# Redistributing K, Q and the selection mask inside the chip, instead of by extra reads of PSUM and by transfers

## The chip, the core and the metric

The kernel runs on one core of a Trainium2 chip. The metric is the device time of the program in microseconds, where less is better. [...] An instruction that waits for a semaphore holds all that follows it on its engine.

## What is computed

For 4 batches and 8 heads of width 64 over 768 positions, each query picks 6 of 24 chunks of 32 keys by an upper bound on its scores, and attends causally to those alone. The heads side by side then go through a two-layer network with an ELU between its layers.

```python
k_min = np.min(k_chunks, axis=3); k_max = np.max(k_chunks, axis=3)
ub = sum_d(maximum(q * k_min, q * k_max))          # per query and chunk
ub = where(causal, ub, -1e9); top_chunks = argsort(ub)[..., -6:]
scores = where(selected & causal, q @ k.T / 8, -1e9)
attn = softmax(scores); x = heads_side_by_side(attn @ v)     # 3072 x 512
h = x @ w_in                                       # 512 -> 2048
out = where(h > 0, h, exp(min(h, 0)) - 1) @ w_out  # 2048 -> 512
```

## The kernel before

The work is cut into eight units (batch b, half h of the sequence), in the order (0,0), (0,1), (1,0) and so on. A unit has four head pairs r. For each pair `prep` loads K, Q and V of the half (384 positions, both heads side by side in the free dimension), transposes K and Q on PE so that head 0 lies in partitions 0 to 63 and head 1 in 64 to 127 of a PSUM bank (`tr`, L383), and reduces the K bank to the chunk minima and maxima (`red`, two reductions on DVE, L392).

The scores need one operand per head with the mask beside it. `lhsA` holds K of head 0 in the lower 64 partitions and constant mask rows (`econst`, -40000 where a key's chunk is the row's chunk) in the upper 64. `lhsB` holds K of head 1 in the upper half and mask rows in the lower one. `rhsA` and `rhsB` hold Q in the same way with a 0/1 row per chunk, one where the chunk is not selected, so that one product of 128 rows gives the masked scores. K and Q are written straight from PSUM: `ka`, `kb`, `qa`, `qb` (helper `evac`, L404 on ACT, L406 on DVE), and Q a third time as a float copy `qt` (L438) with its positive part `qr` (L443, DVE) for the upper bound. A bank that one engine reads is not read by another at the same time, so the reductions on DVE and the evacuations on ACT of one bank take turns.

`select` works on two pairs. PE forms the bounds (L468) from `qt`, `qr` and `kst`, the padded minima and differences that POOL writes in 4 small instructions per pair (L418, L422). DVE transposes (L478), takes the eight largest of each query (`max`, L487), compares (L493) and transposes back (L499) into `selT`. Four transfers on the SP queue then bring the rows of `selT` to the partitions where `rhsA` and `rhsB` want them.

`attend` forms scores (L530), exponentials (ACT, L542, L548), the triangular mask on the diagonal blocks (DVE, L557, L565), the product with V (L584), the normalisation (DVE, L595, L598), a transpose (L609) and a copy to `xt` (DVE, L614). `mlp` takes the four `xt` of a unit: 16 blocks of the first layer on PE (L626), exp on ACT (L634), `m` on POOL (L638), `gT` on DVE (L642), then the second layer on PE (L653), a copy out of PSUM (L661, L663) and the store.

What is issued when is set by a list scheduler in the program: every operation has costs on the engines that may do it and a priority, `Graph.run` walks a model of the engines, and the instructions are emitted in the order found. Attention of a unit has priorities spread over 10 or 19 units of model time, and the MLP of unit i starts at 14 + 15.1 i, so MLP blocks and later attention are interleaved. Loads are issued ahead on SP, in the same order list; a weight chunk is loaded from POOL after a given cast of V (L451, POOL).

Ahead of all that `consts` sets up the identity, the triangle, the mask rows and the tiles. On DVE this is 39 instructions: 8 memsets of `kst`, 8 copies of mask rows into `lhsA` and `lhsB` (L299, POOL does 8 more) and 20 memsets of the mask halves of `rhsA` and `rhsB` among them.

Of the kernel before, what the change touches and what calls it, by code (L numbers as in the profile page):

```python
# [19 lines left out]
S = 768  # L20
# [32 lines left out]

# [6 lines left out]
class Graph:  # L60
# [40 lines left out]
    def run(self, dma_lat=(700.0, 1300.0)):  # L101
        free = {n: [(0.0, s) for s in range(len(v))] for n, v in self.slots.items()}
        engines = (PE, ACT, DVE, POOL, SP)
        at = {e: 0.0 for e in engines}
        avail = {e: [] for e in engines}
        events = [0.0]
# [9 lines left out]
        while left:  # L116
# [12 lines left out]
            while moved:  # L129
                moved = False  # L130
                for e in engines:
# [5 lines left out]
                    while i < len(lst):  # L137
# [27 lines left out]
                    for b in o.bufs:  # L165
# [48 lines left out]
def kernel(  # L214
# [24 lines left out]
    slots("kf", 6, [P, 3, 2, D], F32)  # L239
    slots("qf", 6, [P, 3, 2, D], F32)  # L240
    slots("vf", 6, [P, 3, 2, D], F32)
    slots("lhsA", 8, [P, S], BF16)
    slots("lhsB", 8, [P, S], BF16)
    slots("vext", 8, [P, 6, 2, D + 1], BF16)
    for h in range(2):
        slots(f"rhsA{h}", 5, [P, HS], BF16)
        slots(f"rhsB{h}", 5, [P, HS], BF16)
    slots("kst", 8, [P, 2, 64], F32)
# [19 lines left out]
    econst = const.tile([P, NCH, CHUNK], BF16, name="econst")  # L268
# [9 lines left out]

    def consts():
        nc.gpsimd.memset(ident_f, 0.0)  # L280
        nc.gpsimd.affine_select(out=ident_f, in_=ident_f, compare_op=AOT.not_equal,
                                fill=1.0, base=0, pattern=[[-1, P]], channel_multiplier=1)
        nc.vector.memset(warm, 0.0)
        nc.scalar.activation(out=warm, in_=warm, func=AF.Exp)
        nc.vector.memset(econst, MASKNEG)
        for r0 in (0, 64):
            nc.gpsimd.affine_select(out=econst[r0:r0 + 64], in_=econst[r0:r0 + 64],
                                    compare_op=AOT.is_equal, fill=0.0, base=0,
# [3 lines left out]
                                fill=0.0, base=0, pattern=[[1, P]], channel_multiplier=-1)  # L292
        nc.vector.tensor_copy(out=ident_b, in_=ident_f)
        for t in store["kst"]:
# [31 lines left out]
    for i in range(8):  # L326
        att_at.append(att_at[-1] + ATT_W[i % 2])
    W_GATE = [2, 3, 4, 5, 6, 7, 8, 9]
# [15 lines left out]
    vx = {}  # L344
    qq = {}
    ks = {}
    xT = {}

    def dma(dst_src, writes, reads, prio, xfer, name):
        def emit(e):  # L350
            d, s_ = dst_src()
            nc.sync.dma_start(out=d, in_=s_)
        g.op(name, c_dma(), emit, reads=reads, writes=writes, prio=prio, xfer=xfer)

    def load(b, h, r, prio):
        kf, qf, vf = g.buf("kf"), g.buf("qf"), g.buf("vf")
        for buf, src, late in ((kf, k, 0.0), (qf, q, 0.001), (vf, v, 3.0)):
            for hd in range(2):
                dma(lambda buf=buf, src=src, hd=hd: (
                        ap(buf)[:, :, hd, :],  # L360
                        src[b, 2 * r + hd, HS * h:HS * (h + 1)].rearrange("(n p) d -> p n d", p=P)),
                    [(buf, hd)], [], prio + late, 440.0, f"ld{b}{h}{r}")
        return kf, qf, vf

    def prep(b, h, r, prio):
# [32 lines left out]
        g.op("kmax" + tag, c_dve(HS), red(1, AOT.max), reads=[(bank, 0)], writes=[(kmm, 1)], prio=prio)  # L398

        def evac(eng_prio, dst, rows, cols, bk, n=HS, src0=0, name="ev"):  # L400
            def emit(e):
                o, i = ap(dst)[rows, cols], ap(bk)[rows, src0:src0 + n]
                if e == ACT:
                    nc.scalar.activation(out=o, in_=i, func=AF.Copy)  # L404
                else:
                    nc.vector.tensor_copy(out=o, in_=i)  # L406
# [314 lines left out]
```

## Time and profile before

| | |
|---|---|
| time, median of 3 runs | 331.62 us (330.03 to 333.14) |
| profiled execution | 331.95 us, its span 330.2 us |
| PE busy | 290.7 us, 88% of the span |
| DVE, ACT, POOL busy | 215.5, 213.8, 125.1 us |
| mean granted clock of PE | 0.984 |
| moved by transfers | 30.70 MB |

The span is the time from the first to the last instruction that the profiler recorded; 1.75 us of the profiled time lie around it. Busy shares are means over a start in which PE mostly waits and a long middle in which it hardly does, so the table by stretches in the section of rows says more than this one. "Idle" beside a group of instructions is the time that their engine stood still just before them, with what ended it.

### The profile page before, as it was taken

To read this page: it belongs to the slowest core of one execution; us is meant where nothing else is said; L and a number is where in the kernel's file an instruction comes from. 1 tells how busy PE (TensorE), PEld (TensorE's weight loads), DVE (VectorE), ACT (ScalarE), POOL (GpSimd) and SP (SyncE) were. 2 spreads that over 40 slices of the span, in tenths; PEclk is the share of its full clock that TensorE was granted. 3 is DMA by queue.
4 is the path that set the end of the run, shared out by engine and by line. 5 is a ranking of instruction groups with operands and counts; after the bars stand their busy time and mean duration, and the time that the engine had idled before them with its cause. 6 is when DMAs were issued, how large, how long until landed. Compare 5 with 4: busy or idle time off the path is not lost.

```text
span 330.2 us, 6933 instructions
## 1 busy us (share of the span) xinstructions
PE 290.7 (88%) x2272; PEld 172.8 (52%) x2272; DVE 215.5 (65%) x652; ACT 213.8 (65%) x477; POOL 125.1 (38%) x324
## 2 busy tenths in 40 slices
PE   4066468868999999999999999999999999999995
PEld 2044154534566656655566556656556556555542
DVE  7855877636459984686558972777589926951640
ACT  2055466943878828779759847898588685781722
POOL 8635442735136711464024600443134412520630
PEclk9997979997999999999999999999999999999999
DMA  6834999895748454504152213222110020000102
GB/s 138 186 81 76 217 195 222 149 194 118 179 108 233 106 129 119 127 9 98 47 151 53 52 48 91 65 60 48 70 37 2 2 73 32 11 2 34 64 2 95
DMA packets 86820, 30.70 MB, mean 93 GB/s; under 512 B 78848, under 2 KB 83712, under 8 KB 86784
## 3 DMA queue, kind: packets, MB, share of 16 engines
q1 hardware_dynamic: 82560, 26.07, 32.2%
q0 software_dynamic: 4224, 4.19, 8.0%
q8 instruction: 18, 0.29, 0.4%
q14 instruction: 18, 0.15, 0.2%
HBM read 27.26 MB, written 6.29 MB: 102 GB/s over the span
## 4 chain that ended last, share of the span: by engine, by line
PE 59%; DVE 16%; ACT 12%; DMA 5%; issue 4%; POOL 2%; SPq 1%; DVEq 0%; ACTq 0%; POOLq 0%
PE bank L653 23%; PE bank L626 16%; PE bank L530 6%; PE bank L383 5%; PE bank L584 4%; ACT pt L542 4%; PE bank L468 4%; DVE kmm L392 3%; DMA vf<-in_v_dram 3%; DVE gT L642 2%; DMA kf<-in_k_dram 2%; PE bank L609 2%; ACT e L634 2%; ACT lhsA L404 1%; ACT rhsA L404 1%
## 5 line engine op out<-in xcount | busy, mean ns | idle before, releaser
L626 PE MATMUL bank<-xt,w_in_sb 128*128 128x384 bf16 x512 | 94.8, 329 | 0.4 <-ACT pt L542 0.3
L638 POOL TENSOR_SCALAR m<-e 128x384 f32<-128x384 f32 x128 | 64.8, 517 | 79.7 <-ACT e L634 70.6
L653 PE MATMUL bank<-w_out_sb,gT 128*128 128x512 bf16 x384 | 93.9, 382 | 0.1
L542 ACT ACTIVATE pt<-bank 128x384 bf16<-128x384 f32 (+1 forms) x160 | 75.2, 577 | 12.4 <-PE bank L530 12.3
L642 DVE SCALAR_TENSOR_TENSOR gT<-bank,m 128x384 bf16<-128x384 f32 x128 | 67.3, 546 | 23.9 <-POOL m L638 22.2
L634 ACT ACTIVATE e<-bank 128x384 f32<-128x384 f32 x128 | 61.7, 516 | 22.1 <-PE bank L626 12.0
L626 PEld LDWEIGHTS <-w_in_sb 128*128 128x128 bf16 x512 | 48.8, 98 | 30.7 <-issue 3.4
L653 PEld LDWEIGHTS <-gT 128*128 128x128 bf16 x384 | 36.2, 98 | 36.2 <-issue 3.0
L418 POOL COPY kst<-kmm 64x12 f32<-64x12 f32 x64 | 12.6, 198 | 86.3 <-DVE kmm L392 71.6
L392 DVE TENSOR_REDUCE kmm<-bank 128x12 f32<-128x384 f32 x64 | 34.6, 551 | 14.6 <-ACT lhsA L404 9.4
L530 PE MATMUL bank<-rhsB,lhsB 128*128 128x384 bf16 x144 | 36.0, 294 | 2.0 <-DVE gT L642 0.8
L530 PE MATMUL bank<-rhsA,lhsA 128*128 128x384 bf16 x144 | 36.6, 296 | 0.9 <-DVE gT L642 0.3
L404 ACT ACTIVATE lhsA<-bank 64x384 bf16<-64x384 f32 x31 | 15.2, 491 | 23.7 <-PE bank L383 22.4
L661 ACT ACTIVATE o<-bank 128x512 f32<-128x512 f32 x20 | 11.9, 596 | 28.6 <-PE bank L653 28.5
L584 PEld LDWEIGHTS <-pt 128*128 128x128 bf16 x672 | 24.6, 97 | 9.9 <-issue 2.7
L584 PE MATMUL bank<-vext,pt 128*128 128x65 bf16 x672 | 26.9, 194 | 2.1 <-DVE pt L565 1.3
L404 ACT ACTIVATE lhsB<-bank 64x384 bf16<-64x384 f32 x30 | 14.6, 485 | 19.8 <-DVE kmm L392 18.3
L468 PE MATMUL bank<-qt,kst 128*64 128x192 f32 (+1 forms) x64 | 14.1, 448 | 14.3 <-POOL kst L418 11.9
L557 DVE TENSOR_TENSOR pt<-pt,tri 128x512 bf16<-128x512 bf16 x32 | 13.8, 432 | 17.9 <-ACT pt L542 17.9
L383 PE MATMUL bank<-ident_f,kf 128*128 128x128 f32 x96 | 18.6, 309 | 5.9 <-DMA kf<-in_k_dram 5.8
L530 PEld LDWEIGHTS <-lhsA 128*128 128x128 bf16 x144 | 14.2, 100 | 13.3 <-issue 4.9
L422 POOL TENSOR_TENSOR kst<-kmm 64x12 f32<-64x12 f32 x64 | 14.4, 224 | 15.8 <-DVE kmm L392 11.1
(55 smaller groups left out, 307.9 us busy)
## 6 DMA issues: line engine op xcount, KB each, us to landing
kf<-in_k_dram SPq DMA_DIRECT2D x64, 96.0 KB
qf<-in_q_dram SPq DMA_DIRECT2D x64, 96.0 KB
vf<-in_v_dram SPq DMA_DIRECT2D x64, 96.0 KB
out_dram<-o SPq DMA_DIRECT2D x24, 256.0 KB
w_in_sb<-in_moe_w_in_dram POOLq DMA_DIRECT2D x4, 512.0 KB, 7.3
w_out_sb<-in_moe_w_out_dram POOLq DMA_DIRECT2D x4, 512.0 KB, 7.2
rhsA<-selT SPq DMA_DIRECT2D x16, 18.0 KB
rhsB<-selT SPq DMA_DIRECT2D x16, 18.0 KB
```

The lines of the kernel that those rows point to most:

```text
L383: nc.tensor.transpose(ap(bk)[:, P * n:P * (n + 1)], ap(src)[:, n], ident_f)
L392: nc.vector.tensor_reduce(out=ap(kmm)[:, w, :], in_=ap(bank)[:, 0:HS].rearrange("p (c w) -> p c w", w=CHUNK), axis=AX.X, op=op)
L404: nc.scalar.activation(out=o, in_=i, func=AF.Copy)
L468: nc.tensor.matmul(ap(bank)[64 * j:64 * j + 64, 0:nq], lhsT=ap(ks[b, r])[:, w, :], rhs=ap(qq[b, h, r][w])[:, 0:nq], start=(w == 0), stop=( ...
L530: nc.tensor.matmul(ap(banks[hd])[:, o + pc:o + pc + wd], lhsT=ap(ls[hd])[:, P * kb:P * (kb + 1)], rhs=ap(rs[hd])[:, c0 - HS * h:c0 - HS * ...
L542: lambda e, hd=hd, pt=pt, banks=banks, wtot=wtot: nc.scalar.activation(out=ap(pt)[:, hd, 0:wtot], in_=ap(banks[hd])[:, 0:wtot], func=AF.Ex ...
L584: nc.tensor.matmul(o3v()[:, hd, qi, :], lhsT=ap(pt)[:, hd, P * qi + off:P * qi + off + P], rhs=ap(vx[b, r])[:, kb, hd, :], start=(kb == 0) ...
L626: nc.tensor.matmul(ap(bank)[:, 0:HS], lhsT=w_in_sb[:, kk, P * fc:P * (fc + 1)], rhs=ap(xT[b, h, kk]), start=(kk == 0), stop=(kk == NKK - 1))
L634: lambda e, eb=eb, bank=bank: nc.scalar.activation(out=ap(eb), in_=ap(bank)[:, 0:HS], func=AF.Exp),
L638: lambda e, eb=eb, mb=mb: nc.gpsimd.tensor_scalar(out=ap(mb), in0=ap(eb), scalar1=-1.0, scalar2=1.0, op0=AOT.add, op1=AOT.mult),
L642: lambda e, gt=gt, bank=bank, mb=mb: nc.vector.scalar_tensor_tensor(out=ap(gt), in0=ap(bank)[:, 0:HS], scalar=0.0, in1=ap(mb), op0=AOT.max ...
L653: nc.tensor.matmul(ap(bank), lhsT=ap(gts[fc])[:, P * tt:P * (tt + 1)], rhs=w_out_sb[:, fc, :], start=(fc == 0), stop=(fc == NFC - 1))
```

## The change

Six things change together.

- K and Q are read from PSUM once each, by `kt` and `qt` (all 128 partitions, ACT or DVE). Four copies per pair of 64 partitions each, SBUF to SBUF, then put K and Q of both heads into the lower partitions of one tile per pair (`lhs`, `rhs`, with a head index): `ka` on DVE or POOL, `qa` on DVE, POOL or ACT. The mask rows lie in the upper half for both heads, offset by 32 rows for head 1.
- The selection rows go from `selT` into `rhs` by one DVE copy per pair (`mk`), which shifts partitions and writes both heads. The four transfers per `select` are gone.
- `kst` is made by one subtraction (`ks`) and one multiplication with a 0/1 column (`kp`) for both heads, on DVE or POOL.
- K, Q and V of batches 1 to 3 are loaded for the whole sequence, V of both heads in one transfer and cast in one instruction. The first two Q loads are issued by ACT.
- The setup is shorter: mask rows are written into `lhs` once for each of 8 slots (`ec`, DVE), 5 memsets of `rhs` and 2 of `selb` stay on DVE, those of `kst` go to POOL, and PE gets 28 matmuls of zeros at the start.
- The scheduler starts each engine at a given time, keeps two engines from one bank at the same time, and has other costs for some operations.

```diff
-    def run(self, dma_lat=(700.0, 1300.0)):
+    def run(self, at=None, dma_lat=(900.0, 1500.0)):
...
-        at = {e: 0.0 for e in engines}
+        at = {e: (at or {}).get(e, 0.0) for e in engines}
...
+                            elif b.cls == "bank" and any(x != e and ft > t for x, ft in b.used.items()):
                                 ok = False
...
-    slots("kf", 6, [P, 3, 2, D], F32)
+    slots("kf", 3, [P, 6, 2, D], F32)
...
-    slots("lhsA", 8, [P, S], BF16)
-    slots("lhsB", 8, [P, S], BF16)
+    slots("kt", 3, [P, HS], BF16)
+    slots("lhs", 8, [P, 2, S], BF16)
...
     def consts():
+        nc.vector.memset(zeros, 0.0)
...
+        for i in range(FILL):
+            nc.tensor.matmul(store["bank"][7][:, 0:P], lhsT=zeros, rhs=zeros, start=True, stop=True)
...
+        for t in store["rhs0"]:
+            nc.vector.memset(t[up, :, 0:Q0], 0.0)
+        for t in store["kst"]:
+            nc.gpsimd.memset(t, 0.0)
...
-        for i in range(8):
-            eng = nc.vector if i < 4 else nc.gpsimd
-            for t, r in ((store["lhsA"][i], slice(64, P)), (store["lhsB"][i], slice(0, 64))):
-                eng.tensor_copy(out=t[r, :], in_=econst[r].rearrange("p c w -> p (c w)"))
...
+    FILL = 28
+    AT = {PE: 3500.0, ACT: 800.0, DVE: 3200.0, POOL: 6000.0, SP: 800.0}
...
+        elif h == 0:
+            dma(lambda: (ap(vf).rearrange("p g n d -> p (g n) d"),
+                         v[b, 2 * r:2 * r + 2].rearrange("g s d -> (g s) d")
+                         .rearrange("(m p) d -> p m d", p=P)),
...
+                g.op("ec" + tag, {DVE: (480, 560)}, ec, writes=[(lb, "e")],
...
-        evac(prio + 0.5, la, lo, ts, bank, name="ka")
-        evac(prio + 0.5, lb, hi, ts, bank, name="kb")
...
+        put("kt", lambda: ap(kt), lambda: ap(bank)[:, 0:HS], c_both(HS), [(bank, 0)], [(kt, 0)], prio)
+        for hd, rows in enumerate((lo, hi)):
+            put("ka", lambda hd=hd: ap(lb)[lo, hd, ts], lambda rows=rows: ap(kt)[rows],
+                {DVE: (175, 260), POOL: (500, 560)}, [(kt, 0)], [(lb, (h, hd))], prio + 0.5)
...
+        g.op("ks" + tag, {DVE: (85, 160), POOL: (200, 260)}, sub, reads=[(kmm, 0)], writes=[(kmm, 1)],
...
+        g.op("kp" + tag, {DVE: (115, 190), POOL: (250, 310)}, pad, reads=[(kmm, 0), (kmm, 1)],
...
-        evac(prio + 0.5, ra, lo, slice(0, HS), bq, name="qa")
-        evac(prio + 0.5, rb, hi, slice(0, HS), bq, name="qb")
...
+            put("qa", lambda hd=hd: ap(rb)[lo, hd], lambda rows=rows: ap(qt)[rows],
+                {DVE: (275, 360), POOL: (500, 560), ACT: (386, 480)}, [(qt, 0)], [(rb, hd)], prio + 0.5)
...
-            dma(lambda ra=ra, j=j: (ap(ra)[64:64 + NCH, q0:HS], ap(sT)[64 * j:64 * j + NCH, 0:nq]),
-                [(ra, "mask")], [(sT, 0)], prio, 60.0, "mk" + tag)
...
+                eng.tensor_copy(out=ap(rb)[hi, :, q0:HS],
+                                in_=ap(sT)[64 * j:64 * j + 64, 0:nq].rearrange("p (a q) -> p a q", a=1)
+                                .to_broadcast([64, 2, nq]))
+            g.op("mk" + tag, {DVE: (2 * nq / 3.84 + 75, 2 * nq / 3.84 + 160)},
...
-    order = g.run()
+    order = g.run(AT)
```

The order of the instructions moves at three places that matter below. The first is DVE from the start of the program to its first reduction of a K bank. Before:

```order
L285 MEMSET econst 128x768
L295 MEMSET kst_131 128x128
...
L299 COPY lhsA_87<-econst 64x768
L299 COPY lhsB_95<-econst 64x768
...
L302 MEMSET rhsA_111 64x192
...
L304 MEMSET rhsB_130 64x192
L392 TENSOR_REDUCE kmm_139<-bank_61 128x12 x2
L406 CAST rhsA_111<-bank_62 64x384
L443 TENSOR_SCALAR qr_146<-qt_142 128x192
```

Now, where `rhs`, `lhs` and `qt` are the new tiles:

```order
L296 MEMSET econst 64x768
L297 MEMSET econst 64x768
L300 MEMSET half 128x2
...
L311 MEMSET rhs_97 64x2x96
...
L316 MEMSET selb_130 128x192
L316 MEMSET selb_131 128x192
L418 COPY lhs_81<-econst 64x1536
...
L418 COPY lhs_87<-econst 64x1536
L492 TENSOR_SCALAR qr_122<-qt_118 128x192
L454 TENSOR_REDUCE kmm_115<-bank_62 128x12 x2
L418 COPY lhs_88<-econst 64x1536
L476 TENSOR_TENSOR kst_107<-kmm_115,half 128x4x12
```

The 8 copies of half a tile and 30 memsets ahead of the first reduction became 7 copies of twice the size and 14 memsets.

The second place is ACT on the first head pairs, where it shares the K and Q banks (61 to 64) with DVE. Before:

```order
L404 ACTIVATE lhsA_87<-bank_61 64x384
L404 ACTIVATE lhsB_95<-bank_61 64x384
L438 ACTIVATE qt_142<-bank_62 128x192
L404 ACTIVATE rhsB_116<-bank_62 64x384
L404 ACTIVATE lhsA_88<-bank_63 64x384
L404 ACTIVATE lhsB_96<-bank_63 64x384
```

Now:

```order
L441 ACTIVATE qt_118<-bank_61 128x384
L441 ACTIVATE kt_78<-bank_62 128x384
L441 ACTIVATE rhs_97<-qt_118 64x384
L441 ACTIVATE qt_119<-bank_63 128x384
L441 ACTIVATE kt_79<-bank_64 128x384
L441 ACTIVATE rhs_98<-qt_119 64x384
```

ACT reads each K bank once where it read it twice, and the third instruction of a pair reads SBUF.

The third place is the SP queue at the first two selections. Before:

```order
L352 DMA rhsA_112<-selT_156 24x192
L352 DMA rhsB_117<-selT_156 24x192
L352 DMA vf_86<-in_v_dram 128x3x64 x2
L352 DMA kf_69<-in_k_dram 128x3x64 x2
L352 DMA qf_75<-in_q_dram 128x3x64 x2
L352 DMA rhsA_113<-selT_157 24x192
L352 DMA rhsB_118<-selT_157 24x192
```

Now, at the end of batch 0 and the start of batch 1:

```order
L369 DMA qf_72<-in_q_dram 128x3x64 x2
L369 DMA vf_75<-in_v_dram 128x3x64 x2
L369 DMA kf_70<-in_k_dram 128x6x64 x2
L369 DMA qf_73<-in_q_dram 128x6x64 x2
L369 DMA vf_76<-in_v_dram 128x12x64
L369 DMA kf_71<-in_k_dram 128x6x64 x2
```

No transfer on SP reads `selT` any more; until the first store it holds loads alone.

## Rows read from the trace of the kernel before

**Rows 1.** The page's busy times: engine, us, share of the span, instructions.
```profile
PE 290.7 (88%) x2272; PEld 172.8 (52%) x2272; DVE 215.5 (65%) x652; ACT 213.8 (65%) x477; POOL 125.1 (38%) x324
```

**Rows 2.** Table by stretches: window, length, busy us, granted PE clock, DMA share, GB/s.
```profile
0.00:14.50 14.50, 3.34 (x12) 2.01 (x12) 12.13 (x39) 1.97 (x3) 11.11 (x28) 1.00 0.70 158
14.50:31.00 16.50, 10.01 (x41) 6.64 (x42) 9.48 (x36) 8.04 (x19) 5.99 (x23) 0.91 0.37 79
31.00:54.30 23.30, 14.71 (x122) 8.75 (x121) 18.04 (x54) 14.02 (x30) 10.07 (x26) 0.92 1.18 207
54.30:90.00 35.70, 29.83 (x219) 16.86 (x217) 20.28 (x63) 22.41 (x53) 15.29 (x35) 0.95 0.83 166
90.00:306.60 216.60, 212.66 (x1780) 128.17 (x1778) 146.62 (x446) 157.60 (x355) 74.67 (x198) 1.00 0.27 71
```

**Rows 3.** Timeline of the first 20 us: start, us, engine, line, what.
```profile
3.92 0.44 DVE L299 COPY lhsA<-econst 64x768 bf16<-64x768 bf16 x1 [0.94 <-POOL econst L287]
4.08 0.87 PE L383 MATMUL bank<-ident_f,kf 128*128 128x128 f32 x3 [4.08 <-DMA kf<-in_k_dram]
4.38 0.35 DVE L299 COPY lhsB<-econst 64x768 bf16<-64x768 bf16 x1
4.58 0.84 POOL L299 COPY lhsA<-econst 64x768 bf16<-64x768 bf16 x1
4.74 0.89 DVE L299 COPY lhsA<-econst 64x768 bf16<-64x768 bf16 x1
...
14.54 0.48 DVE L392 TENSOR_REDUCE kmm<-bank 128x12 f32<-128x384 f32 x1
```

**Rows 4.** Groups of DVE, 0 to 14.5 us: busy, mean ns of one, idle before.
```profile
L302 DVE MEMSET rhsA<- 64x192 uint32 x10 | 2.1, 218 | 0.2
L295 DVE MEMSET kst<- 128x128 f32 x8 | 1.1, 165 | 0.0
L285 DVE MEMSET econst<- 128x768 bf16 x1 | 0.7, 698 | 0.1
```

**Rows 5.** Groups of DVE, 14.5 to 54.3 us.
```profile
L392 DVE TENSOR_REDUCE kmm<-bank 128x12 f32<-128x384 f32 x17 | 9.4, 553 | 7.7 <-ACT lhsA L404 4.9 <-ACT lhsB L404 2.8
L406 DVE CAST rhsA<-bank 64x384 bf16<-64x384 f32 x5 | 2.7, 542 | 0.0
L406 DVE CAST rhsB<-bank 64x384 bf16<-64x384 f32 x3 | 1.7, 560 | 0.1
L443 DVE TENSOR_SCALAR qr<-qt 128x192 f32<-128x192 f32 x4 | 1.1, 281 | 0.0
L595 DVE RECIPROCAL rcp<-bank 128x6 f32<-128x6 f32 x4 | 0.7, 171 | 0.0
L598 DVE TENSOR_TENSOR on<-bank,rcp 128x384 bf16<-128x384 f32 x4 | 2.2, 548 | 0.0
```

**Rows 6.** Timeline of the SP queue, 14 to 48 us: two issues that follow each other.
```profile
17.78 1.03 SPq L352 DMA_DIRECT2D qf<-in_q_dram  x2
24.77 0.89 SPq L352 DMA_DIRECT2D rhsA<-selT  x1
```

**Rows 7.** Timeline, 44 to 86 us: the first MLP, and POOL's wait for V.
```profile
54.34 4.18 PE L626 MATMUL bank<-xt,w_in_sb 128*128 128x384 bf16 x24
...
72.23 0.51 POOL L451 TENSOR_SCALAR vext<-vf 128x384 bf16<-128x384 f32 x1 [4.83 <-DMA vf<-in_v_dram]
75.34 0.34 PE L609 MATMUL bank<-ident_b,on 128*128 128x128 bf16 x3 [4.29 <-DVE on L598]
```

**Rows 8.** Chain that ended last: start, us, what.
```profile
100.29 1.30 PE bank L626 x8
265.90 1.63 PE bank L530 x12
```

**Rows 9.** Groups of the whole run, POOL.
```profile
L422 POOL TENSOR_TENSOR kst<-kmm 64x12 f32<-64x12 f32 x64 | 14.4, 224 | 15.8 <-DVE kmm L392 11.1 <-PE bank L530 0.9 <-PE bank L626 0.8
L638 POOL TENSOR_SCALAR m<-e 128x384 f32<-128x384 f32 x128 | 64.8, 517 | 79.7 <-ACT e L634 70.6 <-DVE gT L642 5.0 <-DVE kmm L392 0.6
```

More of the change, by code (lines that the diff above doesn't have):

```diff
@@ L267 @@
     tri01 = const.tile([P, P], BF16, name="tri01")
-    econst = const.tile([P, NCH, CHUNK], BF16, name="econst")
+    econst = const.tile([P, 2, NCH, CHUNK], BF16, name="econst")
+    half = const.tile([P, 2], F32, name="half")
+    zeros = const.tile([P, P], BF16, name="zeros")
     warm = const.tile([P, 1], F32, name="warm")
@@ L282, in consts @@
                                 fill=1.0, base=0, pattern=[[-1, P]], channel_multiplier=1)
[L283 to L288, printed above, removed]
+        nc.vector.memset(econst[up, 0], MASKNEG)
+        nc.vector.memset(econst[up, 1], MASKNEG)
+        for i in range(FILL):
+            nc.tensor.matmul(store["bank"][7][:, 0:P], lhsT=zeros, rhs=zeros, start=True, stop=True)
+        nc.vector.memset(half, 0.0)
+        nc.vector.memset(half[0:64, 0:1], 1.0)
+        nc.vector.memset(half[up, 1:2], 1.0)
+        for hd in range(2):
+            nc.gpsimd.affine_select(out=econst[up, hd], in_=econst[up, hd],
+                                    compare_op=AOT.is_equal, fill=0.0, base=32 * hd,
                                     pattern=[[1, NCH], [0, CHUNK]], channel_multiplier=-1)
@@ L347, with dma @@
     xT = {}
[L349 removed]
+    lo, hi = slice(0, 64), slice(64, P)
+    g.op("table", {ACT: (1300, 1300)}, lambda e: nc.scalar.activation(out=warm, in_=warm, func=AF.Exp),
+         prio=-90.0)
+    def dma(dst_src, writes, reads, prio, xfer, name, eng=SP, issue=490.0):
         def emit(e):
             d, s_ = dst_src()
[L352 to L353 removed]
+            (nc.scalar if e == ACT else nc.sync).dma_start(out=d, in_=s_)
+        g.op(name, {eng: (issue, issue)}, emit, reads=reads, writes=writes, prio=prio, xfer=xfer)
@@ L398, in prep @@
         g.op("kmax" + tag, c_dve(HS), red(1, AOT.max), reads=[(bank, 0)], writes=[(kmm, 1)], prio=prio)
[L400 to L406, printed above, removed]
-            return g.op(name + tag, c_both(n), emit, reads=[(bk, 0)], writes=[(dst, (h, rows.start))],
-                        prio=eng_prio)
@@ L410, in prep @@
[L410 to L425 removed]
+        kt = g.buf("kt")
@@ new lines, in cast @@
+        def cast(name, ks_, cost, keys):
+            casts.append(g.op(
+                name, cost,
+                lambda e: nc.gpsimd.tensor_scalar(
+                    out=ap(vx[b, r])[:, ks_, :, 0:D].rearrange("p k g d -> p g k d"),
+                    in0=ap(vf)[:, :, ks_], scalar1=1.0, scalar2=0.0, op0=AOT.mult, op1=AOT.add),
+                reads=[(vf, key) for key in keys], writes=[(vx[b, r], hh) for hh in {k_[0] for k_ in keys}],
+                prio=prio + 3.0))
+        if b == 0:
+            cast("v" + tag, slice(3 * h, 3 * h + 3), {POOL: (520, 580)}, [(h, 0), (h, 1)])
+        elif h == 0:
+            cast("v" + tag, slice(0, 6), {POOL: (850, 910)}, [(hh, hd) for hh in range(2) for hd in range(2)])
```

178 lines of the change are left out of this document (105 added, 73 removed).

## The prediction

> **What bounds the kernel now.** I read the busy times first, then the table by stretches, then the timeline of the first 90 us. The busy times name PE, with 290.7 us of 330.2 [rows 1]. The table shows that this is an average over two regimes [rows 2]. From 90 to 306.6 us PE is busy for 212.66 of 216.6 us, and there 8 matmuls of the first layer take 1.30 us, 0.163 us each for 384 columns [rows 8], so PE runs at its pace and 3.9 us of idle time are all that a better order could win. Ahead of 54.3 us PE is busy for 28 us only, and 54.34 us is where the first MLP block starts [rows 7]. What ends last before that is mostly DVE. It is in setup until 14.54 us, while the first K transposes were done at about 5 us [rows 3]. Then it is busy for 9.48 + 18.04 = 27.5 of 39.8 us [rows 2], and 7.7 of the 12.3 idle us lie just ahead of the chunk reductions, ended by ACT, which reads the same K bank in between [rows 5]. So the start is a chain through DVE, the middle is PE, and an engine that gets less work in the middle gives nothing back.
>
> **Setup on DVE.** Out go 20 memsets of 0.218 us (4.3 us) and 8 of 0.165 (1.1) [rows 4], 8 copies of mask rows (0.44 + 0.35 + 6 x 0.89 = 6.1) and the 0.94 us in which the first of them waited for POOL [rows 3], 12.4 in all. In come 7 memsets as wide as one of the 0.218 us (1.5), a second `econst` memset (0.7, half the partitions but as many elements), four small memsets (0.5, taken below the 0.165 us of 128 elements), one `qr` ahead of the reduction (0.28, [rows 5]) and 7 copies of 1536 elements. The trace has copies of 768: 0.35 us with POOL not copying, 0.89 while POOL copies too [rows 3]. In the new start POOL has memsets there, so I take twice 0.35, 0.70 each, 4.9 in all; the ends are 0.35 (2.5) and 1.78 (12.5). The first reduction moves from 14.54 to 14.54 - 12.4 + 7.9 = 10.0 us. [...]
>
> **From there to the first MLP block.** DVE's list in this stretch loses 8 evacuations from PSUM (2.7 + 1.7) and one reduction (0.55), and gains two `qt` copies (0.55 each, as the casts). It holds more attention and one selection less, which I count as +1.3: one `on` (0.55), one reciprocal (0.17), three triangle products and two `xt` copies more, a 384-wide transpose and two `qr` less, the latter near 0.4 each. New are 17 instructions: 6 `mk`, 4 `kp`, 3 `ks`, 2 `qa`, 1 `ka` and the last `ec`. No row shows them; the nearest are 0.17 us (a reciprocal of 6 elements) and 0.56 (a cast of 64x384 from PSUM) [rows 5], and I take 0.30, near the 192-wide `qr`, 5.1 in all with ends of 2.9 and 9.5. Busy time becomes 27.5 - 4.4 - 0.55 + 1.1 + 1.3 + 5.1 = 30.1. Of the idle time the 7.7 us go, since ACT reads a K bank once, ahead of both reductions. Late next is the subtraction `ks`, which POOL does for the first pairs: `kp` waits on DVE, and behind it the next pair's `qr` and reductions. The nearest row is POOL's 0.224 us for 12 columns [rows 9]; three waits of 0.3 make 0.9. So 4.6 + 0.9 = 5.5 idle, 35.6 us in all, and the first MLP block starts at 45.6 instead of 54.34: **8.7 us**. PE has by then also done 24 score matmuls more than before; 12 take 1.63 us [rows 8], so **3 us** of its later work are gone. The other differences on PE up to there (30 small products with V more, one bound less) nearly cancel.
>
> **The queue.** SP issued no load between 18.81 and 24.77 us, because a mask transfer that waited for `selT` stood at its head [rows 6]. That is gone, with the issue of 64 mask transfers (0.89 us for the one shown). The mask itself comes by `mk`, priced above, and nothing has to land. Later POOL waited 4.83 us for a V tile with the MLP's `m` behind it, DVE and PE behind that, and PE stood for 4.29 us [rows 7]; the stretch from 54.3 to 90 us has 35.7 - 29.8 = 5.9 us of PE idle [rows 2]. With loads issued earlier I give it half, **3 us**, with ends of 0 and 5.9, since V of batch 1 now comes in pieces four times as large.
>
> **What costs nothing, and its cover.** POOL gets 80 half copies (0.42 each, half of 0.84 [rows 3]; 34 us) and 36 small operations (8 us), memsets of `kst` (1.3 at DVE's price), and loses 128 small operations (28 at 0.22 each) and 8 copies (6.7): about 9 us more on 125, covered by the 79.7 us that it waits ahead of `m` [rows 9]; without the cover each copy in front of an `m` delays a `gT` by 0.4. ACT's list becomes shorter (53 reads of PSUM and 40 half copies in place of 135 reads); it is busy for 213.8 of 330 us [rows 1] with PE as the bound, so that is no gain. Whole-sequence loads move the same bytes: batch 0 needs 48 loads of 96 KB, 23 us at 207 GB/s [rows 2], its four weight chunks 2.1 MB or 10 us more, 33 of 45.6 us. The 28 zero matmuls fall into the time before the first loads land, 4.08 us [rows 3]; if they take twice that long, the reductions still start at 10.0. The four Q loads on ACT come ahead of its table load, also under the setup.
>
> **The sum.** 8.7 + 3 + 3 = 14.7 off the profiled 331.95 us (span 330.2 and 1.75 around it) gives 317.3. The median of the runs is 0.33 lower, so 317.
>
> **Rivals.**
> First, DVE and POOL get in each other's way. A DVE copy took 0.35 us alone and 0.89 beside POOL's copies, about the length of POOL's own 0.84 [rows 3], and the change puts SBUF copies on both. If that holds throughout, the 7 `ec` cost 12.5 instead of 4.9 (+7.6) and ten of the new copies in the chain 0.5 more each (+5): 317 + 12.6 = 330, no change. Against it: POOL does memsets while the `ec` run. [...] Chance 0.10.
> Second, the waits move instead of going. The idle share of DVE stays at 12.3 us, because pads, bounds and first scores follow each other in a denser chain, and the V wait stays. That is 6.8 + 3 us less: 327. For it: 4.6 of the 12.3 idle us have causes that no part of this change touches, and a shorter list leaves less to fill waits with. Chance 0.14.
> Third, **slower**: POOL's queue. V casts of a whole sequence stand among the `m` operations, and a cast that waits holds them all. Each such wait as long as the one in the trace costs PE 4.3 us. There are 12 whole-sequence casts; with four long waits the gain is gone, with six it is 317 + 3 + 6 x 4.3 = 346. For it: the wait was there with pieces a quarter as large. Against it: the transfers are busy for 0.27 of the time after 90 us [rows 2], so V can be early there. Chance 0.08.
> Fourth, better: the new operations cost 0.17 (-2.2), DVE does not wait (-5.5), the whole 5.9 go (-2.9): 306. Chance 0.12.
>
> **How the numbers follow.** The forecast of 317 has the remaining 0.56, with 311 to 323 as its own range from the ends of the copies and of the new operations. The range of 306 to 329 takes in the fourth and second cases and part of the first, and leaves out the slower one. About 1%, 3.3 us, is what a measurement of this kernel can tell from no change. Faster than 328.3 are the forecast, the fourth case and most of the second, 0.80; the first and the rest of the second lie within 1%, 0.12; slower, 0.08.
>
> **What would show it.** [...] The middle should keep PE at 98% busy. The prediction is wrong if the first MLP block starts before 40 or after 52 us, or if PE's idle time after 90 us moves by more than 4 us either way.

## The result and the profile after

The changed kernel takes 319.97 us (median of 4 runs, 317.75 to 321.54) against 331.58 for the kernel before: a ratio of 0.9645, 95% interval 0.9564 to 0.9725, so 11.6 us faster. 317 was forecast, with a range of 306 to 329. The total is right; several of the reasons are not, as the experiments show.

In these kernels PE forms the matrix products and PEld loads their weights, DVE, ACT and POOL copy, reduce and evaluate functions, and SP issues transfers. Busy times and the table by stretches of the changed kernel, as in [rows 1, 2]. Its trace lacks 22 of the 384 products of the second layer, so PE is a little understated after 90 us.

```profile
PE 293.0 (92%) x2278; PEld 177.5 (56%) x2300; DVE 229.0 (72%) x687; ACT 201.5 (63%) x438; POOL 142.1 (44%) x298
```
```profile
0.00:14.50 14.50, 8.69 (x48) 6.47 (x48) 12.89 (x31) 6.41 (x12) 9.09 (x34) 1.00 0.83 176
14.50:31.00 16.50, 12.77 (x71) 7.42 (x72) 12.13 (x40) 5.84 (x12) 9.41 (x18) 0.90 1.05 193
31.00:54.30 23.30, 17.65 (x146) 11.29 (x145) 17.01 (x63) 16.66 (x39) 10.84 (x21) 0.85 1.13 197
54.30:90.00 35.70, 32.97 (x278) 20.28 (x281) 29.70 (x93) 23.78 (x53) 20.86 (x40) 1.00 0.75 140
90.00:306.60 216.60, 211.69 (x1696) 128.03 (x1713) 156.68 (x463) 147.06 (x322) 91.81 (x188) 1.00 0.25 63
```

The middle is as before (PE idle 4.9 us of 216.6, before 3.9). Summed up to 90 us, PE is busy for 72.1 us where it was busy for 57.9 (mean granted clock 0.94 in both); less the 3.2 us of zeros that is 11.0 us more, 7.9 of it by 54.3 us, and there the 11.6 us are won. From 54.3 to 90 us PE idles for 2.7 us instead of 5.9, and the transfers are busy from 14.5 us on (share 1.05 where it was 0.37). But DVE still idles for 39.8 - 29.14 = 10.7 us from 14.5 to 54.3 us, where it idled for 12.3. Its groups there, busy | idle before, as in [rows 5]:

```profile
L454 DVE TENSOR_REDUCE kmm<-bank 128x12 f32<-128x384 f32 x14 | 7.3, 546 | 0.5 <-PE bank L435 0.4
L618 DVE TENSOR_TENSOR pt<-pt,tri 128x512 bf16<-128x512 bf16 x6 | 2.6, 438 | 1.9 <-ACT pt L603 1.9
L443 DVE COPY qt<-bank 128x384 f32<-128x384 f32 x2 | 1.1, 558 | 1.6 <-PE bank L435 1.6
L536 DVE STREAM_TRANSPOSE ubT<-bank 128x192 f32<-128x192 f32 x2 | 0.8, 383 | 2.6 <-PE bank L525 2.5
L536 DVE STREAM_TRANSPOSE ubT<-bank 128x384 f32<-128x384 f32 x1 | 0.6, 582 | 3.1 <-PE bank L525 3.1
```

The 7.7 us ahead of the reductions have become 0.5, and DVE waits for PE's bounds (5.7), the exponentials (1.9) and Q (1.6) instead. Timeline of the changed kernel: the zeros, the places of [rows 3, 7], and the longest bounds:

```profile
1.06 3.17 PE L299 MATMUL bank<-zeros 128*128 128x128 bf16 x28 [1.06 <-DVE warm L292]
...
4.80 5.66 DVE L418 COPY lhs<-econst 64x1536 bf16<-64x1536 bf16 x7
10.65 1.01 DVE L454 TENSOR_REDUCE kmm<-bank 128x12 f32<-128x384 f32 x2
...
26.55 1.79 PE L525 MATMUL bank<-qt,kst 128*64 128x384 f32 x3
...
51.44 1.07 PE L687 MATMUL bank<-xt,w_in_sb 128*128 128x384 bf16 x4
...
54.48 5.37 PE L687 MATMUL bank<-xt,w_in_sb 128*128 128x384 bf16 x32
```

The first reduction is at 10.65 us (10.0 forecast), two reductions stand back to back, and the first MLP block is at 51.44 (45.6 forecast), 2.9 us earlier than before where 8.7 were forecast. Steady MLP work starts at 54.48 only, no earlier than before (54.34).

### The profile page after: what moved, and what is told of

Read it like the earlier page. It is cut to its first block, busy times and chain, and to the rows that moved or that the text cites. A ratio compares the mean times of both kernels' runs of the same rounds, so it can differ in the third digit from the quotient of the medians.

```text
span 319.6 us, 6664 instructions
## 1 busy us (share of the span) xinstructions
PE 293.0 (92%) x2278; PEld 177.5 (56%) x2300; DVE 229.0 (72%) x687; ACT 201.5 (63%) x438; POOL 142.1 (44%) x298
## 4 chain that ended last, share of the span: by engine, by line
PE 56%; DVE 35%; ACT 3%; issue 2%; POOL 2%; POOLq 0%; ACTq 0%; DVEq 0%
PE bank L714 23%; PE bank L687 13%; PE bank L591 9%; DVE gT L703 8%; DVE kmm L454 5%; PE bank L645 4%; PE bank L525 4%; DVE thr L545 3%; PE bank L435 2%; DVE rhs L565 2%; DVE lhs L418 2%; ACT pt L603 2%; DVE kst L476 2%; DVE qr L492 2%; DVE ubT L536 2%
## 5 line engine op out<-in xcount | busy, mean ns | idle before, releaser
L714 PE MATMUL bank<-w_out_sb,gT 128*128 128x512 bf16 x362 | 91.4, 379 | 1.1
L591 PE MATMUL bank<-rhs,lhs 128*128 128x384 bf16 (+2 forms) x288 | 55.5, 302 | 10.8 <-DVE rhs L565 6.3
L445 POOL COPY lhs<-kt 64x384 bf16<-64x384 bf16 x59 | 31.8, 540 | 27.5 <-ACT kt L441 25.0
L591 PEld LDWEIGHTS <-lhs 128*128 128x128 bf16 x288 | 26.9, 101 | 27.7 <-issue 11.8
L441 ACT ACTIVATE kt<-bank 128x384 bf16<-128x384 f32 x29 | 14.5, 500 | 15.7 <-PE bank L435 13.1
L445 POOL CAST rhs<-qt 64x384 bf16<-64x384 f32 x21 | 11.3, 538 | 28.8 <-ACT qt L441 19.9
L525 PE MATMUL bank<-qt,kst 128*64 128x192 f32 (+1 forms) x64 | 17.5, 474 | 6.3 <-DVE kst L476 6.2
L618 DVE TENSOR_TENSOR pt<-pt,tri 128x512 bf16<-128x512 bf16 x32 | 14.6, 455 | 10.7 <-ACT pt L603 10.7
L441 ACT ACTIVATE rhs<-qt 64x384 bf16<-64x384 f32 x40 | 20.8, 521 | 1.5 <-DVE qt L443 0.9
L609 ACT ACTIVATE pt<-bank 128x512 bf16<-128x512 f32 x32 | 19.5, 608 | 1.9 <-PE bank L591 1.8
L435 PE MATMUL bank<-ident_f,qf 128*128 128x128 f32 x96 | 17.6, 298 | 1.0 <-POOL tri L308 0.6
```

Of the source, the lines that this page charges most:

```text
L441: nc.scalar.activation(out=dst(), in_=src(), func=AF.Copy)
L445: nc.gpsimd.tensor_copy(out=dst(), in_=src())
L525: nc.tensor.matmul(ap(bank)[64 * j:64 * j + 64, 0:nq], lhsT=ap(ks[b, r])[:, w].rearrange("p h c -> p (h c)"), rhs=ap(qq[b, h, r][w])[:, q0 ...
L591: nc.tensor.matmul(ap(banks[hd])[:, o + pc:o + pc + wd], lhsT=ap(ls)[:, hd, P * kb:P * (kb + 1)], rhs=ap(rs)[:, hd, c0 - HS * h:c0 - HS * ...
L714: nc.tensor.matmul(ap(bank), lhsT=ap(gts[fc])[:, P * tt:P * (tt + 1)], rhs=w_out_sb[:, fc, :], start=(fc == 0), stop=(fc == NFC - 1))
```

## The experiments

Medians, and ratios to the kernel before on the same chip. An edit of an operation, a cost or a rule makes the scheduler plan anew, so most rows compare two orders as well; `no_pool_spare` (against `no_pool`), `setup_long` and `warm` keep the order.

| kernel | us | ratio, 95% interval |
|---|---|---|
| the change | 320.0 | 0.9645 (0.9564 to 0.9725) |
| `u_masks`: masks by transfers again | 329.1 | 0.9915 (0.9879 to 0.9951) |
| `u_evac`: K and Q from PSUM per head again | 311.8 | 0.9407 (0.9376 to 0.9437) |
| `k_evac`: K alone so | 315.0 | 0.9528 (0.9486 to 0.9569) |
| `no_pool`: half copies not on POOL | 312.7 | 0.9444 (0.9405 to 0.9482) |
| `no_pool_spare`: that, and idle copies on POOL | 319.2 | 0.9651 (0.9609 to 0.9693) |
| `u_loads`: loads by halves again | 316.9 | 0.9564 (0.9530 to 0.9598) |
| `setup_long`: 4.4 us more setup on DVE | 322.4 | 0.9720 (0.9680 to 0.9759) |
| `warm`: products of zeros in the start | 327.8 | 0.9900 (0.9854 to 0.9945) |
| `p_masks`: before, masks copied by DVE | 331.1 | 1.0012 (0.9987 to 1.0037) |
| `p_sched0`: before, new scheduler rules | 324.7 | 0.9796 (0.9756 to 0.9835) |
| `p_masks_sched`: before, both | 316.4 | 0.9561 (0.9518 to 0.9603) |
| `best_evac`: three undone or altered parts | 313.8 | 0.9492 (0.9453 to 0.9530) |

### Undoing one part: the masks

```diff
-            g.op("mk" + tag, {DVE: ...}, mk, reads=[(sT, 0)], writes=[(rb, "mask")], ...)
+            for hd in range(2):
+                dma(lambda ...: (ap(rb)[hi, hd, q0:HS], ap(sT)[64 * j:64 * j + 64, 0:nq]),
+                    [(rb, "mask")], [(sT, 0)], prio, 60.0, "mk" + tag)
```

> The changed kernel with its masks brought by transfers on the SP queue again (two per pair, 64 rows each) in place of the DVE copies mk. Theory (the queue counts): each mask transfer waits at the head of SP's queue for selT, so the hole in the loads near 20 us is back (4 us or more without an issue), POOL waits 3 us or more for a V tile between 54 and 90 us, and the transfer's landing (about 2 us) stands in the chain ahead of the first scores; DVE is freed of some 2.5 us in the start. Time 322 to 326. Rival (the queue term came from other parts, the hole is covered): the time stays within 1.5 us of 320, with or without a hole.

Measured: 329.1, so 9 us are lost, more than expected. SP's queue in this kernel (start, us, what):

```profile
14.28 0.49 SPq L369 DMA_DIRECT2D vf<-in_v_dram  x1
18.68 0.54 SPq L369 DMA_DIRECT2D rhs<-selT  x1
19.31 1.06 SPq L369 DMA_DIRECT2D kf<-in_k_dram  x2
```

and what PE waited for up to 90 us (in total, times, longest):

```profile
PE bank L525 <- DVE kst L476: 9.6, 7, 3.2
PE bank L435 <- DMA qf<-in_q_dram: 8.1, 4, 4.5
PE bank L435 <- DMA kf<-in_k_dram: 5.3, 3, 2.9
```

A mask transfer holds the queue for 3.9 us, later loads start later, and PE waits 13.4 us for K and Q, against 0.4 in the changed kernel. POOL's wait for a V tile is there too, one of 9.0 us; what share of the 9 us each wait has was not separated. Two more things moved, so not all of the 9 us need be the queue itself. The scheduler planned another order: up to 90 us PE ran 374 other products and only 32 of the first MLP layer, while the changed kernel starts that layer after 254 products and has run 79 of it by 90 us. And PE's granted clock is lower, 0.60 and 0.62 in two stretches where the changed kernel has 0.90 and 0.85:

```profile
14.50:31.00 16.50, 10.66 (x38) 5.72 (x39) 12.61 (x47) 4.80 (x10) 9.51 (x19) 0.60 0.88 164
31.00:54.30 23.30, 13.24 (x79) 8.65 (x76) 11.84 (x48) 7.81 (x16) 8.72 (x19) 0.62 1.09 193
```

### Undoing one part: K and Q from PSUM once

```diff
-        put("kt", lambda: ap(kt), lambda: ap(bank)[:, 0:HS], c_both(HS), ...)
-            put("ka", ..., lambda rows=rows: ap(kt)[rows], {DVE: (175, 260), POOL: (500, 560)}, ...)
+            put("ka", ..., lambda rows=rows: ap(bank)[rows, 0:HS], c_both(HS), [(bank, 0)], ...)
...
-            put("qa", ..., lambda rows=rows: ap(qt)[rows], {DVE: ..., POOL: ..., ACT: ...}, ...)
+            put("qa", ..., lambda rows=rows: ap(bq)[rows, 0:HS], c_both(HS), [(bq, 0)], ...)
```

> The changed kernel with K written from PSUM once per head again (ka from the bank, no kt), and Q read from its bank three times (qt and two qa), the rest as changed. The theory of the prediction (reading each bank once ends the waits ahead of the reductions): DVE's idle time between the first reduction and the first MLP block rises by 5 to 8 us, and the time rises by 4 to 7 us, to 324 to 327. Rival (the waits only moved to other places, and DVE's list in the start gets shorter without the half copies): the time stays within 2 us of 320, and DVE's idle time in the start stays at 10 to 13 us.

Measured: 311.8. Both theories missed it: the time falls by 8 us, and DVE's idle time from the first reduction (9.05 us) to the first MLP block (47.07) is 6.3 us. The reductions of this kernel from 14.5 to 54.3 us, though ACT and DVE read each K bank twice beside them and not once:

```profile
L454 DVE TENSOR_REDUCE kmm<-bank 128x12 f32<-128x384 f32 x15 | 7.9, 549 | 0.1
```

No wait ahead of the reductions came back, so the single read was not needed to end it. The single read itself, as the change does it, costs time.

### Why the single read costs: POOL's copies

`k_evac` is the K half of the edit above. `no_pool` keeps `kt` and `qt`:

```diff
-                {DVE: (175, 260), POOL: (500, 560)}, [(kt, 0)], ...
+                {DVE: (175, 260)}, [(kt, 0)], ...
-                {DVE: (275, 360), POOL: (500, 560), ACT: (386, 480)}, [(qt, 0)], ...
+                {DVE: (275, 360), ACT: (386, 480)}, [(qt, 0)], ...
```

> The changed kernel with the half copies of K (ka) on DVE alone and those of Q (qa) on DVE or ACT, none on POOL; kt and qt stay. It asks why writing K and Q from PSUM once per head gained 8 us. Theory 1 (POOL's copies hold DVE's instructions up, and are late): ec is never above 0.65 us, the multiplication kp takes 0.3 us or less on average before 54 us, and the time falls by 4 to 8 us, to 312 to 316. Theory 2 (the second hop from the bank through kt or qt makes the chain longer, whoever does it; DVE now has 59 copies of 0.26 us more, 15 us over the kernel and some 4 us in the start): the time stays within 2 us of 320.

> The changed kernel with K alone written from its bank once per head (no kt), Q still through qt. POOL loses its 59 copies of K and keeps the 21 or so of Q. Theory 1 (POOL's copies and the hop through kt cost): most of the 8 us that both together gave, 312 to 316. Theory 2 (the gain is Q's, since ACT and DVE no longer wait for qt): 317 to 321.

Measured: 312.7 without POOL's copies, all but 1 us of the 8, although DVE takes 59 copies of K more; 315.0 with K alone changed. Of theory 1's signs the time came out, and `kp` (0.296 us on average before 54 us); the one on `ec` did not, since one of them still took 1.89 us (see the setup below). By the medians the second hop costs about 1 us, the two orders being different, and POOL's part in it is the rest. `no_pool_spare` keeps `no_pool`'s order on every engine and adds scratch copies, and a memset of their source in POOL's setup:

```diff
                 if name == "kt":
+                    for _ in range(2):
+                        nc.gpsimd.tensor_copy(out=econst[lo, 0, 0:12], in_=econst[lo, 1, 0:12])
```

> The changed kernel without copies of K and Q on POOL (312.7 us), its order kept on every engine, and in POOL's list two copies of 64x384 in scratch for each kt, 64 in all, which nobody waits for. Theory 1 (copies on POOL hold DVE's instructions up): ec is back at 0.75 us or more on average, small DVE operations beside these copies are longer, and the time rises by 3 to 6 us, to 316 to 319. Theory 2 (POOL's copies cost because K comes late from them, and because the scheduler put other work in other places): the time stays within 1.5 us of 312.7. Where DVE's durations do not change but the time rises, POOL's queue ahead of ks, kp and m is the reason.

Measured: 319.2, 6.5 us slower through copies that nobody waits for. Neither late K nor another order is thus needed for the loss. DVE's busy time rose from 235.8 to 241.3 us with the same instructions, most of it in `ka`. Its groups, first in `no_pool`, then with the spare copies:

```profile
L443 DVE COPY lhs<-kt 64x384 bf16<-64x384 bf16 x64 | 19.1, 299 | 0.6
```
```profile
L447 DVE COPY lhs<-kt 64x384 bf16<-64x384 bf16 x64 | 23.7, 370 | 0.6
```

The expected sign, longer `ec`, did not show (0.66 us on average against 0.72). Here POOL's setup was slowed beside `ec` instead: its eight memsets of `kst` took 4.11 us, 1.22 in `no_pool`. From the first reduction to the first MLP block DVE has 107 instructions in both kernels (in `no_pool`, then with the spare copies; third number: DVE busy):

```profile
9.72:43.06 33.34, 23.62 (x191) 15.11 (x191) 30.00 (x107) 20.70 (x45) 12.71 (x26) 0.80 1.11 208
```
```profile
9.17:46.45 37.28, 23.25 (x193) 14.36 (x193) 31.96 (x107) 21.28 (x47) 21.45 (x50) 0.83 1.11 203
```

This stretch is 3.9 us longer: half of it is longer instructions on DVE, half is DVE's idle time (3.3 to 5.3 us). Over the whole run PE waits for mask rows from DVE 5.6 us where it waited 2.2, for `kst` from POOL 6.3 where it waited 5.5. How much of the 6.5 us goes back to longer DVE instructions in the end, and how much to POOL's own queue ahead of `ks`, `kp` and `m`, stays open.

### Setup, loads, clock

```diff
+        for t in store["rhs0"] + store["rhs1"]:
+            nc.vector.memset(t[up, 0], 0.0)
+            nc.vector.memset(t[up, 1], 0.0)
```

> The changed kernel with 20 more memsets of 64x384 in DVE's setup (0.22 us each by the kernel before, 4.4 us in all), ahead of the first reduction, nothing else. Theory (the start is a chain through DVE): the first reduction moves from 10.65 to 15.0 us, the first full MLP block from 54.5 to 58 or later, and the time rises by 3.5 to 4.5 us, to about 324. Rival (the start is set by the landing of loads or by PE, and the setup only fills a wait): the time rises by less than 1.5 us.

Measured: 322.4, 2.5 us more, between the two. The 20 memsets took their 4.2 us, yet the first reduction came only 1.87 us later:

```profile
8.94 3.39 DVE L421 COPY lhs<-econst 64x1536 bf16<-64x1536 bf16 x7
12.35 0.26 DVE L495 TENSOR_SCALAR qr<-qt 128x192 f32<-128x192 f32 x1
12.52 1.01 DVE L457 TENSOR_REDUCE kmm<-bank 128x12 f32<-128x384 f32 x2
```

The seven `ec` took 3.39 us instead of 5.66, since POOL's setup memsets and its first three copies (4.6 to 7.6 us) now ran beside memsets of DVE. In the changed kernel POOL does this beside the `ec`:

```profile
4.60 1.23 POOL L313 MEMSET kst<- 128x128 f32 x8
5.77 0.53 POOL L318 MEMSET vext<- 128x12 bf16 x8
6.25 0.81 POOL L445 CAST rhs<-qt 64x384 bf16<-64x384 f32 x1
7.02 1.61 POOL L445 COPY lhs<-kt 64x384 bf16<-64x384 bf16 x2
```

The `ec` of the changed kernel, then of `no_pool` (ns, least, median and most), where POOL has the same memsets but no copy before 10 us, and the seven of `no_pool` together:

```profile
L418 DVE COPY lhs<-econst x8: 547/705/1910, 4.8 to 11.7; 64x1536 bf16<-64x1536 bf16 x8
```
```profile
L418 DVE COPY lhs<-econst x8: 542/558/1892, 4.8 to 13.6; 64x1536 bf16<-64x1536 bf16 x8
...
4.79 4.72 DVE L418 COPY lhs<-econst 64x1536 bf16<-64x1536 bf16 x7
```

The longest is the first in both kernels. It starts at 4.8 us, beside POOL's sixteen memsets, and ends 0.4 us after the last of them. So POOL's work had cost the seven `ec` 2.3 us: its memsets 1.3 (4.72 against 3.39), its copies 0.9 (5.66 against 4.72). What delays the first reduction does reach the end, as far as the runs tell: 1.87 us in, the first MLP block 1.37 later (52.81 us), 2.5 out. The intervals of the two kernels overlap a little, and the granted clock from 14.5 to 31 us is lower, 0.60 where the changed kernel has 0.90.

`u_loads` makes the conditions `b == 0` of loads and casts hold for every batch.

> The changed kernel with K, Q and V of every batch loaded by halves and V cast by halves, as batch 0 is; the rest as changed. Theory (the start and the queue's order count, not the number of loads): SP issues 60 loads more, all after batch 0, nothing in the start moves, and the time stays within 1.5 us of 320. Rival (whole-sequence loads are part of the gain, since they free SP and POOL in the middle): 2 us or more slower, with PE's idle time after 60 us larger by as much. Second rival (V in pieces four times as large comes later and holds POOL): 2 us or more faster.

Measured: 316.9, 3 us faster, which the theory did not give. The second rival has this size, but 1.3 us of it is there by the first MLP block (50.10 us), in a start where nothing was to move; its reason was not tested. The intervals (0.9530 to 0.9598, and 0.9564 to 0.9725) overlap a little. Whole-sequence loads bring nothing, and may cost up to 3 us.

`warm` puts products of zeros ahead of others on PE:

```diff
+    def hot(bk, n):
+        for _ in range(n):
+            nc.tensor.matmul(ap(bk)[:, 0:P], lhsT=zeros, rhs=zeros, start=True, stop=True)
```

> The changed kernel, its order untouched, with products of zeros of 128 columns more on PE in the start: 24 ahead of each of the four bound computations of batch 0, 12 ahead of each K and Q transpose of the second half, 24 ahead of the first scores of each pair in batch 0. They write a bank that the next products overwrite. Theory (part of the start is PE at a granted clock of 0.5, in stretches at 26 to 30 and 34 to 40 us): the clock stays at 1.0 up to 54 us, the 8 bound products of the second half take 1.6 us or less in place of 3.66, and the time falls by 3 to 5 us. Rival (PE waits for DVE there, and a faster product only waits longer): the time stays within 1.5 us of 320 although the clock is up. A third outcome is that the zeros stand in the way: slower by 1 us or more.

Measured: 327.8, the third outcome. The bounds of the second half ran in 1.51 us at a granted clock of 1.00, but started at 29.52 us instead of 26.55, and the clock fell in other places (0.50 from 10 to 12 and from 16 to 18 us, 0.55 from 36 to 38). The test does not tell what the clock costs.

### One part alone: the square of masks and scheduler

`p_masks`, on the kernel before, has two copies of 24 partitions per pair:

```diff
-            dma(lambda ra=ra, j=j: (ap(ra)[64:64 + NCH, q0:HS], ap(sT)[64 * j:64 * j + NCH, 0:nq]), ...
-            dma(lambda rb=rb, j=j: (ap(rb)[0:NCH, q0:HS], ...
+                nc.vector.tensor_copy(out=ap(ra)[64:64 + NCH, q0:HS], in_=ap(sT)[64 * j:64 * j + NCH, 0:nq])
+                nc.vector.tensor_copy(out=ap(rb)[0:NCH, q0:HS], in_=ap(sT)[64 * j + 32:64 * j + 32 + NCH, 0:nq])
```

> The kernel before with one part of the change alone: the mask rows of selT are copied into rhsA and rhsB by DVE (two copies of 24 partitions per pair) in place of four transfers per selection on the SP queue. Theory (the mask transfers are the largest cost, as putting them back into the changed kernel suggested, 9 us): the hole in the loads at 18.8 to 24.8 us closes, the waits of POOL for a V tile fall below 1 us, and the time falls by 7 to 10 us, to 322 to 325. Rival (without the shorter setup and the new order the start waits for other things anyway): it falls by 4 us or less.

Measured: 331.1, no gain, although the hole in SP's queue is closed (a load every microsecond from 12 to 30 us) and MLP work starts at 44.02 us, ten earlier. So what was won at the start was lost again later.

`p_sched0` replaces the body of `Graph.run`, with these two rules:

```diff
-    def run(self, dma_lat=(700.0, 1300.0)):
+    def run(self, at=None, dma_lat=(900.0, 1500.0)):
...
+                            elif b.cls == "bank" and any(x != e and ft > t for x, ft in b.used.items()):
+                                ok = False
```

`p_masks_sched` has both edits.

> The kernel before with the mask copies on DVE (331.1 us alone) and with the changed scheduler's rules: one engine at a time on a bank, the longer transfer times; engines start at zero as before. Theory (with masks alone the start gained 5 us and PE's idle time after 90 us gave it back, since the order there was planned with two engines on one bank): PE's idle time after 90 us falls by 3 us or more and the time to 324 to 328. Rival (the middle loses to the mask copies on DVE itself): PE's idle time after 90 us stays, and the time stays within 1.5 us of 331.

> The kernel before with the changed scheduler's rules alone (one engine at a time on a bank, longer transfer times, all engines start at zero), its masks by transfers as before. It completes a square with the masks alone (331.1), the rules and masks together (316.4), and the kernel before (330.3). Theory 1 (the two need each other: without transfers that wait in SP's queue the order can be dense, and with one engine on a bank the planned order is the one that runs): 324 to 330. Theory 2 (the rules alone are the gain, the masks do nothing): 315 to 319. Where it comes between, 319 to 324, each has a part.

Measured: 324.7 with the rules alone, 316.4 with both. Table by stretches of the kernel before, of `p_masks`, of `p_sched0` and of `p_masks_sched` (second number: PE busy):

```profile
14.50:54.30 39.80, 24.72 (x161) 15.38 (x162) 27.53 (x89) 22.06 (x48) 16.06 (x48) 0.91 0.85 154
90.00:290.00 200.00, 196.36 (x1643) 119.23 (x1641) 141.18 (x432) 149.75 (x338) 72.45 (x193) 1.00 0.28 74
```
```profile
14.50:54.30 39.80, 27.39 (x182) 16.28 (x183) 26.98 (x97) 25.30 (x56) 15.30 (x43) 0.91 0.99 191
90.00:290.00 200.00, 191.65 (x1539) 115.11 (x1550) 147.75 (x465) 145.02 (x324) 71.28 (x189) 1.00 0.24 65
```
```profile
14.50:54.30 39.80, 25.57 (x170) 16.57 (x171) 27.62 (x103) 22.15 (x47) 16.17 (x48) 0.87 0.99 177
```
```profile
14.50:54.30 39.80, 32.79 (x246) 20.11 (x246) 32.80 (x110) 30.20 (x67) 19.01 (x53) 0.96 1.05 194
90.00:290.00 200.00, 195.82 (x1619) 118.19 (x1618) 145.56 (x458) 147.58 (x326) 70.66 (x186) 1.00 0.24 64
```

With masks alone PE's idle time from 90 to 290 us grows from 3.6 to 8.4 us (11 products are missing from its trace there, so a little less), and its waits for DVE in that stretch are `pt` 2.3, `gT` 2.2, `xt` 1.3 and `on` 1.2. With the rules too it is 4.2. Only both together fill the start: PE 32.79 busy of 39.8 us, where the kernel before had 24.72. Idle time ahead of the 64 reductions over the whole run, in the kernel before and in `p_sched0`:

```profile
L392 DVE TENSOR_REDUCE kmm<-bank 128x12 f32<-128x384 f32 x64 | 34.6, 551 | 14.6 <-ACT lhsA L404 9.4 <-ACT lhsB L404 4.3 <-PE bank L383 0.5
```
```profile
L400 DVE TENSOR_REDUCE kmm<-bank 128x12 f32<-128x384 f32 x64 | 32.8, 544 | 3.2 <-ACT lhsB L412 1.1 <-POOL kst L426 1.0 <-POOL kst L430 0.6
```

So the scheduler's new rules end most of the taking of turns, with K still read three ways. The rule on banks is the likely one of the two; it was not tried without the longer transfer times.

### A combination

`best_evac` is `u_evac` with the loads of `u_loads`, and the mask rows of batch 1 copied later.

> The changed kernel with what the runs so far point to: K and Q written from PSUM per head (311.8 alone), loads and casts of all batches by halves (3 us alone), and the mask rows of the four tiles of batch 1 copied after the reductions of batch 0's second half in place of the setup. The first reduction should come near 7.5 us instead of 9.05. If the three add up: 311.8 - 3 - 1 = 307.8, between 306 and 310. If the loads' gain was in the start's order and not in the loads, 310 to 313.

Measured: 313.8, 2 to 3 us behind `u_evac` alone (by the medians, by the ratios). The first reduction is earlier (8.11 us against 9.05), but the bounds of the second half start at 23.89 us, in `u_evac` at 23.70, and take longer. In `best_evac`, the first lines of the bounds, then two stretches:

```profile
23.89 2.27 PE L527 MATMUL bank<-qt,kst 128*64 128x384 f32 x3
...
25.99 1.86 PE L527 MATMUL bank<-qr,kst 128*64 128x384 f32 x3
```
```profile
24.00:26.00 2.00, 2.00 (x6) 0.45 (x7) 1.08 (x3) 0.00 (x0) 1.46 (x3) 0.52 1.19 248
26.00:28.00 2.00, 2.00 (x8) 0.64 (x5) 0.12 (x1) 0.00 (x0) 0.00 (x0) 0.63 0.55 90
```

and in `u_evac`:

```profile
23.70 0.87 PE L523 MATMUL bank<-qt,kst 128*64 128x384 f32 x4
24.39 0.82 PE L523 MATMUL bank<-qr,kst 128*64 128x384 f32 x4
```

3.96 us at granted clocks of 0.52 and 0.63 against 1.51 at 1.00 (22 to 26 us), with DVE behind them: 2.5 us of a chain. That this is the whole difference was not shown. `u_evac` stays the fastest version.

## Why the prediction was right in the time and wrong in its reasons

**Setup.** 10.65 us instead of 10.0; seven `ec` cost 0.81 each, not 0.70. The 0.70 was near by luck: with POOL at rest they cost 0.48 each (`setup_long`), and what POOL did beside them added the rest, 1.3 us by its memsets and 0.9 by its copies. "POOL does memsets while the `ec` run", which the prediction held against its first rival, was no protection, since the longest `ec` (1.91 us) is the one beside the memsets. Single `kp` on DVE in the changed kernel point the same way: 0.54 and 0.47 us (at 12.36 and 14.69 us) beside POOL's copies, 0.17 (at 17.17) with none beside it. By what mechanism POOL's work lengthens DVE's was not shown. The step holds, a little small.

**From the reduction to the MLP.** This is the step that failed: "the 7.7 us go, since ACT reads a K bank once". They went, but with the scheduler's new rules, which the sum did not price: 1.8 us are left in the same stretch where only the rules are new, and 0.1 where K is read per head again. And they were not won: from the first reduction to the first MLP block DVE was idle for 10.7 us, not 5.5, since the denser list ran into PE's bounds (5.7 us), part of them at a granted clock of 0.50 (27 to 30 us). The second rival had said so. The first MLP block came 2.9 us earlier, not 8.7, and PE had done 7.9 us more work by 54.3 us where the sum, with its 3 us of score products, had 11.7. The busy time came out as forecast (30.1 us from 10.65 to 51.44 us), in part by luck: the 17 new instructions took 0.39 us each and not 0.30, 1.6 us in all, and other terms were that much too large.

**The queue.** 3 us were given, with ends of 0 and 5.9, from one hole and one V wait. Both are gone, though SP now issues nothing from 35.3 to 40.6 us, and PE's idle time from 54.3 to 90 us fell by 3.1 us. But undone in the changed kernel, the masks cost 9 us, with another order in it; added alone they are worth nothing. The mechanism was right, but the size is not a property of the edit: it depends on whether the planned order can use loads that come early.

**What costs nothing.** POOL's 80 half copies were covered by its waits, so the sum had 0 for them. They cost about 7 us (312.7 without, 320.0 with, 319.2 with copies of no use). The cover was counted on POOL alone; the price is paid in longer instructions on DVE and in what stands behind the copies, in shares that stay open. The first rival, DVE and POOL in each other's way, had the first of these, with 12.6 us and a chance of 0.10.

**The sum.** Masks and rules together give 14.5 us (`p_masks_sched`). POOL's copies take back some 7. What lies between `p_masks_sched` and `no_pool` gives about 4 (316.4 to 312.7): the shorter setup, `kt` and `qt`, `ks` and `kp`, the loads, the zeros and the engines' start times, of which only the loads were undone by themselves. That these make up the measured 11.6 bears nothing out, because the 4 are what was left over. The forecast had 14.7, from other sources and with no loss in it: the gains were some 4 us larger than its sum, and the loss of 7 was missing. That the total came within 3 us of 317 is two errors that nearly cancel.

## What to carry to other kernels

An engine's idle time is no cover for copies that make a neighbour's instructions longer: price them on the neighbour and on what stands behind them, memsets too, and test with copies that nobody waits for (here 64 of them on POOL cost 6.5 us). When a change touches the planner together with the data path, vary the two apart: here each of two parts alone gave 7 us or nothing, both together 14.5. A time that comes out as forecast bears out no step of the sum; undoing the parts one by one does.

## What was not expected of the hardware

No version shown here keeps PE's granted clock at 1.00 from 14.5 to 54.3 us (0.86 to 0.96 in the changed kernel, `u_evac`, `no_pool` and the square), and the stretches near 0.5 lie elsewhere each time: 0.50 from 27 to 30 and from 34 to 40 us in the changed kernel, 0.50 from 28 to 34 in `u_evac`, 0.52 and 0.63 in the two halves of 24 to 28 in `best_evac`. Where one meets the bounds on which DVE waits, 8 products of 384 columns take 3.7 us (the changed kernel) and 3.96 (`best_evac`) instead of 1.51 (`u_evac`, `warm`). What brings the fall on is not settled by these runs, and products of zeros did not prevent it: `warm` has 0.90 from 14.5 to 31 us and 0.93 from there to 54.3, the changed kernel 0.90 and 0.85.
